# Retention into a gated feed-forward layer on one core: early decayed values and masks, both state products behind the row transposes, group 1 by halves, chunk 1 placed later

## The chip, the cores and the metric

The kernel runs on one core of a Trainium2 chip. Its engines are TensorE (PE, matrix products and transposes into PSUM), VectorE (DVE), ScalarE (ACT), GpSimd (POOL) and SyncE (SP), which run beside each other and wait for each other through semaphores; sixteen DMA engines move data. The metric is the device time of one execution in microseconds (us); a time given without more is the median of several runs. A profile covers one execution, from the first to the last instruction (its span).

## The reference, cut to what matters

Two layers in a row. The first is a recurrence over 768 positions for 4 batches and 8 heads of width 64; the second is a normalised, gated feed-forward layer (FFN) over the resulting 3072 rows of 512.

```python
# q, k, v: (4, 8, 768, 64); w_gate, w_val: (512, 1536); w_out: (1536, 512)
gamma = 1.0 - 2.0 ** (-5.0 - np.arange(H))
for t in range(S):
    state = gamma * state + outer(k[:, :, t], v[:, :, t])      # (B, H, D, D)
    y[:, :, t] = 1 / sqrt(D) * q[:, :, t] @ state
x = y.transpose(0, 2, 1, 3).reshape(B * S, H * D)
xn = x / sqrt(mean(x * x, axis=-1) + 1e-6) * rms_g
g = xn @ w_gate
out = (g * sigmoid(g) * (xn @ w_val)) @ w_out
```

## The kernel before

The kernel cuts the positions into 6 chunks of 128. Inside a chunk the recurrence becomes products: scores `a = k q^T` under a causal mask, their product with the values, and the query times the state that the earlier chunks left. The values are scaled by a decay (`vp`), the outputs by its inverse. A chunk has 4 batches of 128 rows, so 512 columns (`GT`) of the FFN; two batches are a group (`p` = 0 or 1). The FFN of a chunk is 12 tiles of hidden columns (`gv`) and 4 down-projections (`down`), and the attention of the next chunk is issued between these. The order of the calls is the order on every engine.

Chunk 0 uses masks that hold the decay already, so only its state needs the scaled values. The pieces that matter here:

```python
    ident_i = nc.vector.tensor_scalar(out=ident, in0=off, scalar1=0.0, scalar2=None, op0=ALU.is_equal)
    late_i = nc.vector.tensor_scalar(out=late, in0=offp_f, ...)     # offp comes from GpSimd
    nc.vector.tensor_tensor(out=reach, in0=offp_f, in1=late, op=ALU.add)

    def decays():              # ScalarE: four activations, vd_* scale values, yd_* scale outputs
        nc.scalar.activation(vd_p, va_p, AF.Exp, scale=-1.0, bias=zero)
        # ... vd_n, yd_p, yd_n likewise

    def vp_pair(c, p):         # GpSimd: the decayed values of a group
        nc.gpsimd.tensor_tensor(out=x, in0=u["v"]..., in1=vd_p[:, c]..., op=ALU.mult)

    def kvp(c, p):             # TensorE: 32 small products, the group's state product
        nc.tensor.matmul(u["kv"][b][t, hp * D:hp * D + D], u["k"][r, h, s], u["vp"][r, h, s], ...)

    def state0(p, eng): ...    # kv from PSUM to st_f
    def state_diag(p): ...     # GpSimd: st_f into the diagonal blocks of st_d (zero elsewhere)
    def state1(p): ...         # VectorE: st_f += kv
    def x_pe(c, p, j): ...     # TensorE: transposes of a normed batch;  x_copy: to SBUF
    def tp(c, p, n, a, eng):   # TensorE: transposes of q or k, and a copy
    def y1(p): ...             # TensorE: query times st_d, and masked scores times vp;  y1_out: scaled

    def gv(c, n0, n1, t0, t1): # hidden tiles n0..n1, columns t0..t1: two PSUM banks of products,
        for wt, name in ((wg_b, "g_ps"), (wv_b, "v_ps")):           # silu on ScalarE, times on VectorE
            ...
```

PSUM has eight banks, given out in turn; once `split[0]` is set, four go to the attention and four to the FFN. The order of chunk 0 and 1 (cut):

```python
    v_cast(0)
    # ... transposes of group 1's q, y0(0, 0), y0(0, 1)
    squares0(0)
    decays()
    # ... norm of group 0, scores of group 1
    load_w(5, 6)
    load_w(6, 8)
    gv(0, 0, 1, 0, 256)
    # ... gv 1, 2; y0 of group 1
    squares0(1); eps0(1); power(0, 1)
    vp_pair(0, 0)
    gv(0, 3, 4, 0, 256)
    norm0(1)
    gv(0, 4, 5, 0, 256)
    for n in "qk":
        load_pair(1, 0, n)
    load_w(8, 10)
    load_w(10, 12)
    gv(0, 5, 6, 0, 256)
    x_pe(0, 1, 0); x_pe(0, 1, 1); # ... and their copies
    load_pair(1, 0, "v", after=i)
    kvp(0, 0)
    vp_pair(0, 1)
    for p in range(2):
        nc.gpsimd.memset(st_d[p], 0.0)
    gv(0, 0, 2, 256, 512)
    state0(0, "a")
    for i in range(3):
        load_wo(4 * i, 4 * i + 4)
    gv(0, 2, 4, 256, 512)
    state_diag(0)
    kvp(0, 1)
    # ... VectorE: causal_p, causal (two tensor_scalar)
    gv(0, 4, 6, 256, 512)
    # ... gv 6 to 11, and chunk 1's group 0 between them
    norm(1, 0, 0, 1)
    down(0, 0); down(0, 1)
    x_pe(1, 0, 0); # ... x_copy, x_pe(1, 0, 1), x_copy
    # ... tp(1, 1), vp_pair(1, 1), down(0, 2), ap(1, 1), ap_mask, down(0, 3), t_dma(2, 0), t_dma(2, 1)

    steps = [L(gv, 1, n, n + 2, t, t + 256) for t in (0, 256) for n in (0, 2, 4, 6)]
    steps += [L(gv, 1, n, n + 1, 0, GT) for n in range(8, NFF)]
    steps += [L(down, 1, b) for b in range(B)]
    y1(1); y1_out(1); kvp(1, 1)
    split[0] = True
    run(steps, {...})          # step number -> attention of chunk 2, issued after that step
    for c in range(2, NCH):
        steps = [L(gv, c, n, n + 1, 0, GT) for n in range(NFF)]
        ...
```

Of the kernel before, what the change touches and what calls it, by code (L numbers as in the profile page):

```python
# [16 lines left out]
def kernel(  # L17
# [11 lines left out]
    nc = tc.nc  # L29
# [10 lines left out]
    GT = B * C  # L40
# [36 lines left out]
    def load_w(n0, n1):  # L77
        sl = slice(n0 * 128, n1 * 128)
        nc.gpsimd.dma_start(out=wg_b[:, :, sl], in_=wg_v[:, :, sl])
        nc.gpsimd.dma_start(out=wv_b[:, :, sl], in_=wv_v[:, :, sl])  # L80
# [62 lines left out]
    mhalf = const.tile([128, 2], F32, name="mhalf")  # L143
    nc.vector.memset(mhalf, -0.5)
    ident = const.tile([128, 128], BF16, name="ident")
    ident_i = nc.vector.tensor_scalar(out=ident, in0=off, scalar1=0.0, scalar2=None, op0=ALU.is_equal)

    late = const.tile([128, 256], F32, name="late")
    offp_f = offp.rearrange("p e f j -> p (e f j)")
    late_i = nc.vector.tensor_scalar(out=late, in0=offp_f, scalar1=0.0, scalar2=1.0e7, op0=ALU.is_lt, op1=ALU.mult)  # L150
    reach = const.tile([128, 256], F32, name="reach")
    nc.vector.tensor_tensor(out=reach, in0=offp_f, in1=late, op=ALU.add)


    mask0 = [[work.tile([128, 2, 256], F32, name="mask0", tag="v_f", bufs=6) for i in range(2)] for a in range(2)]
# [29 lines left out]
    def decays():  # L185
        nc.scalar.activation(vd_p, va_p, AF.Exp, scale=-1.0, bias=zero)
        nc.scalar.activation(vd_n, va_n, AF.Exp, scale=-1.0, bias=zero)
        nc.scalar.activation(yd_p, ya_p, AF.Exp, scale=1.0, bias=lnscale)
        nc.scalar.activation(yd_n.rearrange("p c i a -> p c a i"), va_n.rearrange("p c (a i) -> p c a i", i=2),
                             AF.Exp, scale=1.0, bias=lnscale)  # L190

    causal_p = const.tile([128, 256], BF16, name="causal_p")
    causal = const.tile([128, 128], BF16, name="causal")
    st_f = [const.tile([128, 2, NHP, D], F32, name=f"st_f{p}") for p in range(2)]
    st_b = [const.tile([128, 2, NHP, D], BF16, name=f"st_b{p}") for p in range(2)]

    st_d = [const.tile([128, 2, NHP, 2 * D], BF16, name=f"st_d{p}") for p in range(2)]

    def heat(n):
        hot = bank("hot")  # L200
        for _ in range(n):
            nc.tensor.matmul(hot, ones[:, :128], ones, start=True, stop=True)  # L202
# [49 lines left out]
    def v_cast(p):  # L252
        u = U[0, p]
        u["vb"] = work.tile([128, H, 2 * D], BF16, name="vb", bufs=2)
        nc.scalar.copy(u["vb"], u["v"])

    def vp_pair(c, p):
        u = U[c, p]
        x = work.tile([128, H * 2, D], BF16, name="vp2", bufs=3)
        nc.gpsimd.tensor_tensor(  # L260
            out=x, in0=u["v"].rearrange("p h (e d) -> p (h e) d", e=2),
            in1=vd_p[:, c].rearrange("p h e -> p (h e)")[:, :, None].to_broadcast([128, 2 * H, D]), op=ALU.mult)
        u["vp"] = x.rearrange("p (h e) d -> p h (e d)", e=2)
# [319 lines left out]
    tc_(0, 1, "q", 0, "v")  # L583
    tc_(0, 1, "q", 1, "v")
    squares0(0)
    decays()
    tp(0, 1, "k", 0)
    tp(0, 1, "k", 1)
    eps0(0)
# [25 lines left out]
    squares0(1)  # L615
    eps0(1)
    power(0, 1)
    vp_pair(0, 0)
    gv(0, 3, 4, 0, 256)
    norm0(1)  # L620
    gv(0, 4, 5, 0, 256)
    for n in "qk":
        load_pair(1, 0, n)
    load_w(8, 10)
    load_w(10, 12)
    gv(0, 5, 6, 0, 256)
    x_pe(0, 1, 0)
    x_pe(0, 1, 1)
# [1 line left out]
    i = x_copy(0, 1, 1, "a")  # L630
    load_pair(1, 0, "v", after=i)
    kvp(0, 0)
    vp_pair(0, 1)
    for p in range(2):
        nc.gpsimd.memset(st_d[p], 0.0)
    gv(0, 0, 2, 256, 512)
    state0(0, "a")
    for i in range(3):
        load_wo(4 * i, 4 * i + 4)
    gv(0, 2, 4, 256, 512)  # L640
    state_diag(0)
    kvp(0, 1)
    nc.vector.tensor_scalar(out=causal_p, in0=offp_f, scalar1=0.0, scalar2=None, op0=ALU.is_ge)
    nc.vector.tensor_scalar(out=causal, in0=off, scalar1=0.0, scalar2=None, op0=ALU.is_ge)
    gv(0, 4, 6, 256, 512)
    state0(1, "a")
    vp_pair(1, 0)
    gv(0, 6, 7, 0, GT)
    state_diag(1)
    for n in "qk":  # L650
        load_pair(1, 1, n)
    gv(0, 7, 8, 0, GT)
    for n, e in (("q", "a"), ("k", "v")):
        for a in range(2):
            tp(1, 0, n, a, e)
    load(2, 0)
    i = gv(0, 8, 9, 0, GT)
    load_pair(1, 1, "v", after=i)
    begin(1)
    ap(1, 0, 0)  # L660
    ap(1, 0, 1)
# [3 lines left out]
    kvp(1, 0)  # L665
    ap_mask(1, 0, 1, 0)
    ap_mask(1, 0, 1, 1)
    state1(0)
    gv(0, 10, 11, 0, GT)
    y1(0)  # L670
    gv(0, 11, 12, 0, GT)
    y1_out(0)
# [1 line left out]
    square(1, 0, 1)  # L674
    rstd(1, 0)
    state_cast(0)
    load(2, 1)
    norm(1, 0, 0, 1)
    down(0, 0)
    down(0, 1)  # L680
    x_pe(1, 0, 0)
    x_copy(1, 0, 0, "v")
    x_pe(1, 0, 1)
    x_copy(1, 0, 1, "v")
    for n, e in (("q", "a"), ("k", "v")):
        for a in range(2):
            tp(1, 1, n, a, e)
    vp_pair(1, 1)
    load(2, 2)
    down(0, 2)  # L690
    ap(1, 1, 0)
    ap(1, 1, 1)
    for a in range(2):
# [24 lines left out]
    run(steps, {
        0: [L(square, 1, 1, 0), L(square, 1, 1, 1), L(rstd, 1, 1), L(state1, 1), L(state_cast, 1),
            L(vp, 2, 0), L(vp, 2, 1)],  # L720
        1: [L(norm, 1, 1, 0, 1), L(begin, 2), L(load, 3, 0)],
        2: [L(x_pe, 1, 1, 0), L(x_copy, 1, 1, 0, "v"), L(x_pe, 1, 1, 1), L(x_copy, 1, 1, 1, "a"), L(load, 3, 1),
            L(t_dma, 2, 2), L(t_dma, 2, 3)],
        4: [L(a_pair, 2, 0), L(a_mask, 2, 0, 0)],
        5: [L(a_mask, 2, 0, 1), L(a_mask, 2, 1, 0), L(vp, 2, 2), L(vp, 2, 3)],
        6: [L(a_mask, 2, 1, 1)],
        7: [L(values, 2, 0), L(load, 3, 2), L(t_dma, 3, 0), L(t_dma, 3, 1)],
        8: [L(y_out, 2, 0, 0), L(y_out, 2, 0, 1), L(load, 3, 3)],
        9: [L(state_add, 2, 0), L(a_pair, 2, 1), L(square, 2, 0, 0), L(a_mask, 2, 2, 0)],
        10: [L(a_mask, 2, 2, 1), L(a_mask, 2, 3, 0), L(square, 2, 0, 1), L(rstd, 2, 0), L(state_cast, 0)],  # L730
        11: [L(a_mask, 2, 3, 1), L(norm, 2, 0, 0, 1), L(x_dma, 2, 0, 0), L(x_dma, 2, 0, 1)],
        12: [L(values, 2, 1), L(y_out, 2, 1, 0), L(y_out, 2, 1, 1), L(square, 2, 1, 0), L(square, 2, 1, 1),
             L(rstd, 2, 1), L(norm, 2, 1, 0, 1), L(x_dma, 2, 1, 0), L(x_dma, 2, 1, 1),
             L(state_add, 2, 1), L(state_cast, 1), L(vp, 3, 0), L(vp, 3, 1)],
        13: [L(load, 4, 0), L(t_dma, 3, 2), L(t_dma, 3, 3)],
        14: [L(a_pair, 3, 0), L(a_mask, 3, 0, 0, 1), L(a_mask, 3, 1, 0, 1)],
    })

    for c in range(2, NCH):
        steps = [L(gv, c, n, n + 1, 0, GT) for n in range(NFF)]  # L740
        steps += [L(down_last if (c, b) == (NCH - 1, B - 1) else down, c, b) for b in range(B)]
        d = c + 1
        more = d + 1 < NCH
        more2 = d + 2 < NCH
        after = {}
        if d < NCH:
            after = {
                0: [L(begin, d)] + [L(load, d + 1, 1)] * more,
                1: [L(values, d, 0), L(vp, d, 2), L(vp, d, 3)],
                2: [L(y_out, d, 0, 0)],  # L750
                3: [L(y_out, d, 0, 1)] + [L(state_add, d, 0)] * more,
                4: [L(square, d, 0, 0)],
                5: [L(a_pair, d, 1), L(a_mask, d, 2, 0), L(square, d, 0, 1), L(rstd, d, 0)]
                   + [L(state_cast, 0), L(load, d + 1, 2)] * more,
                6: [L(a_mask, d, 2, 1), L(norm, d, 0, 0), L(x_dma, d, 0, 0)]
                   + [L(t_dma, d + 1, 0)] * more,
                7: [L(norm, d, 0, 1), L(x_dma, d, 0, 1), L(a_mask, d, 3, 0)]
                   + [L(vp, d + 1, 0), L(vp, d + 1, 1), L(t_dma, d + 1, 1)] * more,
                8: [L(a_mask, d, 3, 1)] + [L(load, d + 1, 3)] * more,
                9: [L(values, d, 1)],  # L760
                10: [L(y_out, d, 1, 0)],
                11: [L(y_out, d, 1, 1), L(square, d, 1, 0), L(square, d, 1, 1), L(rstd, d, 1)],
                12: [L(norm, d, 1, 0, 1), L(x_dma, d, 1, 0), L(x_dma, d, 1, 1)]
                    + [L(state_add, d, 1), L(state_cast, 1)] * more
                    + [L(load, d + 2, 0)] * more2 + [L(t_dma, d + 1, 2), L(t_dma, d + 1, 3)] * more,
                13: [L(a_pair, d + 1, 0), L(a_mask, d + 1, 0, 0, 1), L(a_mask, d + 1, 1, 0, 1)] * more,
            }
        run(steps, after)
# [28 lines left out]
```

## Time and profile before

| | before |
|---|---|
| median of 3 runs | 254.52 us (252.93 to 255.78) |
| span of the profiled execution | 252.0 us |
| PE busy | 229.9 us, 91% of the span |
| DVE, ACT, POOL busy | 128.5, 86.6, 116.1 us |
| granted TensorE clock, mean | 0.976 of full speed |
| DMA | 30.48 MB, mean 121 GB/s |

The page shows the span in 40 slices of 6.3 us, with the busy tenths of each engine, and the granted TensorE clock. The list of waits gives, for an instruction's line and the line that released it, the total, the number and the longest. The timeline gives start and duration of instructions, merged where equal ones follow each other; a bracket gives the idle time before, and what ended it. L289 is `kvp`, L260 `vp_pair`, L350 `x_pe`, L517 the products of `gv`, L445 the scores of chunks 2 to 5, L300 `state1`, L496 the addition of the state in later chunks.

### The profile page before, as it was taken

The page shows a single profiled execution, that of the slowest core. Times are in us where ns is not written, and L with a number is a line of the kernel's source. Part 1 is how long each engine was busy: PE and PEld are TensorE (multiplying, and loading weights), DVE is VectorE, ACT ScalarE, POOL GpSimd, SP SyncE. Part 2 cuts the span into 40 slices and gives each one's busy share as a digit, 9 for nine tenths or more (in the row PEclk, how much of TensorE's full clock was granted, in tenths as well). Part 3 has the DMA queues.
Part 4 walks back from the last instruction along what each step waited for, and adds up shares of the span by engine and source line. Part 5 has one row for each costly group of instructions (what it writes and reads, how often), then busy time and mean ns, then how long its engine had stood idle before and what let it go on. Part 6 is the DMA issues. An engine that isn't in the chain of part 4 may idle for free. (4 is left out here: it accounts for less than half of the span.)

```text
span 252.0 us, 5095 instructions
## 1 busy us (share of the span) xinstructions
PE 229.9 (91%) x2050; PEld 122.4 (49%) x2050; DVE 128.5 (51%) x219; ACT 86.6 (34%) x173; POOL 116.1 (46%) x151
## 2 busy tenths in 40 slices
PE   5966839996988999999999999999999999999993
PEld 1444735553576844545454445454444444444442
DVE  2487462566547657464694615675526852144300
ACT  2747403423242332322424133423135323333220
POOL 7945999907929942178391670681400101000000
PEclk9799976999999999999999999999999999999998
DMA  8999999997997999559899499399650103300022
GB/s 102 167 198 156 124 209 194 190 199 92 174 212 101 118 135 170 109 104 158 157 116 176 95 122 194 69 139 125 142 165 3 23 18 82 128 0 0 3 83 85
DMA packets 87799, 30.48 MB, mean 121 GB/s; under 512 B 73696, under 2 KB 83680, under 8 KB 87776
## 3 DMA queue, kind: packets, MB, share of 16 engines
q0 software_dynamic: 53040, 15.21, 62.3%
q1 hardware_dynamic: 34064, 14.82, 30.9%
q8 instruction: 16, 0.26, 0.4%
q10 hardware_dynamic: 672, 0.13, 0.3%
q14 instruction: 7, 0.06, 0.1%
HBM read 28.58 MB, written 6.29 MB: 138 GB/s over the span
## 5 line engine op out<-in xcount | busy, mean ns | idle before, releaser
L522 DVE TENSOR_TENSOR hT<-sg,v_ps 128x512 bf16<-128x512 bf16 (+1 forms) x75 | 49.8, 664 | 82.8 <-PE v_ps L517 80.0
L517 PE MATMUL g_ps<-xnT,wg_b 128*128 128x512 bf16 (+1 forms) x344 | 76.2, 350 | 2.3 <-DVE am L247 0.9
L517 PE MATMUL v_ps<-xnT,wv_b 128*128 128x512 bf16 (+1 forms) x344 | 75.4, 348 | 1.7 <-DMA wv_b<-in_moe_w_val_dram 0.7
L521 ACT ACTIVATE sg<-g_ps 128x512 bf16<-128x512 f32 (+1 forms) x75 | 43.4, 580 | 89.7 <-PE g_ps L517 88.5
L536 PE MATMUL o_ps<-wo_b,hT 128*128 128x512 bf16 x276 | 61.6, 379 | 0.0
L517 PEld LDWEIGHTS <-wv_b 128*128 128x128 bf16 x344 | 33.9, 99 | 31.6 <-DMA wv_b<-in_moe_w_val_dram 1.2
L517 PEld LDWEIGHTS <-wg_b 128*128 128x128 bf16 x344 | 32.5, 99 | 29.2 <-DMA wg_b<-in_moe_w_gate_dram 1.6
L536 PEld LDWEIGHTS <-hT 128*128 128x128 bf16 x276 | 26.5, 98 | 31.6
L414 POOL TENSOR_SCALAR m<-ms 128x2 f32<-128x2 f32 x10 | 2.2, 218 | 77.2 <-ACT xsq L409 77.2
L538 ACT COPY o_sb<-o_ps 128x512 f32<-128x512 f32 x23 | 13.4, 581 | 42.6 <-PE o_ps L536 42.6
L422 DVE SCALAR_TENSOR_TENSOR xn<-x,rstd,g_bc 128x512 bf16<-128x512 f32 x20 | 19.1, 982 | 12.3 <-POOL rstd L330 12.3
L454 DVE TENSOR_TENSOR am<-a_ps,causal 128x512 bf16<-128x512 f32 x32 | 20.9, 682 | 0.0
L428 POOL TENSOR_TENSOR vp<-v_f,vd_n 128x512 bf16<-128x512 f32 x16 | 18.2, 1169 | 0.0
L409 ACT ACTIVATE xsq<-x 128x512 bf16<-128x512 f32 x20 | 12.4, 623 | 9.4 <-DVE x L400 7.7
L104 POOL DMA_DIRECT2D v_f<-in_v_dram x16 | 14.7, 917 | 1.3 <-DMA qb<-in_q_dram 1.3
L107 POOL DMA_DIRECT2D qb<-in_q_dram x16 | 15.0, 937 | 0.1
L107 POOL DMA_DIRECT2D kb<-in_k_dram x16 | 14.4, 899 | 0.0
L400 DVE TENSOR_TENSOR x<-y_ps,yd_n 128x512 f32<-128x512 f32 x16 | 10.8, 684 | 1.1 <-PE y_ps L490 1.1
L202 PE MATMUL hot<-ones 128*128 128x512 bf16 x22 | 7.7, 492 | 1.4 <-DVE ones L135 1.4
L260 POOL TENSOR_TENSOR vp<-v2f,vd_p 128x1024 bf16<-128x1024 f32 x4 | 8.4, 2099 | 0.1
L445 PE MATMUL a_ps<-qT,kT 64*128 64x128 bf16 x128 | 5.9, 218 | 2.4 <-DVE st_f L496 1.8
L308 POOL CAST st_b<-st_f 128x512 bf16<-128x512 f32 x8 | 4.8, 605 | 6.5 <-DVE st_f L496 6.5
(87 smaller groups left out, 160.3 us busy)
## 6 DMA issues: line engine op xcount, KB each, us to landing
v_f<-in_v_dram POOLq DMA_DIRECT2D x16, 256.0 KB, 8.0
out_dram<-o_sb SPq DMA_DIRECT2D x15, 256.0 KB, 2.3
out_dram<-o_sb SPq DMA_DIRECT2D x17, 128.0 KB, 3.9
v2f<-in_v_dram SPq DMA_DIRECT2D x8, 256.0 KB, 5.7
qb<-in_q_dram POOLq DMA_DIRECT2D x16, 128.0 KB, 4.9
kb<-in_k_dram POOLq DMA_DIRECT2D x16, 128.0 KB, 8.0
wo_b<-in_moe_w_out_dram POOLq DMA_DIRECT2D x3, 512.0 KB, 8.8
q2b<-in_q_dram POOLq DMA_DIRECT2D x8, 128.0 KB, 5.1
```

The source lines that it names most:

```text
L104: nc.gpsimd.dma_start(out=x, in_=unit_v[n][c, b])
L107: nc.gpsimd.dma_start(out=x.rearrange("p (h d) -> p h d", h=H), in_=unit_v[n][c, b])
L400: nc.vector.tensor_tensor(out=x[:, :, :, i, :], in0=u["y"][i].rearrange("p (b a d) -> p b a d", b=2, a=NHP), in1=yd_n[:, c, i][:, None, :, ...
L409: nc.scalar.activation(xsq, u["x"][:, b], AF.Square, scale=1.0 / math.sqrt(DM), accum_out=u["ms_"][:, b:b + 1])
L422: nc.vector.scalar_tensor_tensor(out=u["xn"][b], in0=u["x"][:, b], scalar=u["rstd"][:, b:b + 1], in1=g_bc, op0=ALU.mult, op1=ALU.mult)
L428: nc.gpsimd.tensor_tensor(out=x, in0=U[c, b]["v"], in1=vd_n[:, c, :, None].to_broadcast([128, H, D]), op=ALU.mult)
L454: nc.vector.tensor_tensor(out=x, in0=u["a_ps"][i].rearrange("p (a t) -> p a t", a=NHP), in1=causal[:, None, :].to_broadcast([128, NHP, 128 ...
L517: nc.tensor.matmul(x[:, o:o + w], wt[:, s, n * 128:(n + 1) * 128], XT[c][:, s, t0:t1], start=s == 0, stop=s == KS - 1)
L521: nc.scalar.activation(sg[:, :m], ps[0][:, :m], AF.Silu)
L522: return nc.vector.tensor_tensor(out=HT[c][:, n0:n1, t0:t1], in0=sg[:, :m].rearrange("p (n t) -> p n t", t=w), in1=ps[1][:, :m].rearrange( ...
L536: nc.tensor.matmul(ps, HT[c][:, n, b * C:(b + 1) * C], wo_b[:, n, :], start=n == 0, stop=n == NFF - 1)
L538: nc.scalar.copy(o_sb, ps)
```

## The change

Five parts. (1) `decays` and both `vp_pair` calls of chunk 0 are issued earlier, where GpSimd and ScalarE have gaps. (2) The zeros of `st_d` are written by VectorE at the start, in place of GpSimd later, and the two causal masks are made there too. (3) Both state products of chunk 0, `kvp(0, 0)` and `kvp(0, 1)`, follow the row transposes of group 1, and the loads of chunk 1 and of the last weights move up behind them. (4) Chunk 1's FFN is done in halves of 256 columns in all its tiles, and in chunks 2 to 5 the first four tiles are. (5) Chunk 1's work is placed later among the FFN's steps: its row transposes behind a third down-projection, its second group's outputs behind the first FFN step. It is meant to take the waits of TensorE in chunks 0 and 1 off its path.

```diff
+    st_d = [const.tile([128, 2, NHP, 2 * D], BF16, name=f"st_d{p}") for p in range(2)]
+    for p in range(2):
+        nc.vector.memset(st_d[p], 0.0)
     ... late, reach ...
+    nc.vector.tensor_scalar(out=causal_p, in0=offp_f, scalar1=0.0, scalar2=None, op0=ALU.is_ge)
+    nc.vector.tensor_scalar(out=causal, in0=off, scalar1=0.0, scalar2=None, op0=ALU.is_ge)
     ...
     v_cast(0)
+    decays()
+    vp_pair(0, 0)
     ...
     squares0(0)
-    decays()
     ...
     load_w(6, 8)
+    vp_pair(0, 1)
     gv(0, 0, 1, 0, 256)
     ...
     power(0, 1)
-    vp_pair(0, 0)
-    gv(0, 3, 4, 0, 256)
-    norm0(1)
-    gv(0, 4, 5, 0, 256)
     for n in "qk":
         load_pair(1, 0, n)
     load_w(8, 10)
     load_w(10, 12)
+    gv(0, 3, 4, 0, 256)
+    norm0(1)
+    gv(0, 4, 5, 0, 256)
     gv(0, 5, 6, 0, 256)
     ... x_pe, x_copy ...
     kvp(0, 0)
-    vp_pair(0, 1)
-    for p in range(2):
-        nc.gpsimd.memset(st_d[p], 0.0)
+    kvp(0, 1)
     gv(0, 0, 2, 256, 512)
     state0(0, "a")
+    state_diag(0)
     ... load_wo ...
     gv(0, 2, 4, 256, 512)
-    state_diag(0)
-    kvp(0, 1)
-    ... causal_p, causal ...
-    gv(0, 4, 6, 256, 512)
     state0(1, "a")
     vp_pair(1, 0)
+    for n in "qk":
+        load_pair(1, 1, n)
+    gv(0, 4, 6, 256, 512)
     ... v of chunk 1's group 1 is loaded after gv 10 in place of gv 8 ...
     down(0, 0)
+    load(2, 1)
     down(0, 1)
+    vp_pair(1, 1)
+    down(0, 2)
+    ... tp(1, 1) ...
     ... x_pe(1, 0, 0), x_copy, x_pe(1, 0, 1), x_copy ...
-    ... tp(1, 1) ...
-    vp_pair(1, 1)
     load(2, 2)
-    down(0, 2)
     ap(1, 1, 0)
     ...
-    steps = [L(gv, 1, n, n + 2, t, t + 256) for t in (0, 256) for n in (0, 2, 4, 6)]
-    steps += [L(gv, 1, n, n + 1, 0, GT) for n in range(8, NFF)]
+    steps = [L(gv, 1, n, n + 2, t, t + 256) for t in (0, 256) for n in range(0, NFF, 2)]
-    y1(1); y1_out(1); kvp(1, 1)
     run(steps, {
+        0: [y1(1), y1_out(1), kvp(1, 1)],
+        1: [square(1, 1, 0), square(1, 1, 1), rstd(1, 1), state1(1)],
+        2: [begin(2), norm(1, 1), state_cast(1), vp(2, 0), vp(2, 1), t_dma(2, 2), t_dma(2, 3)],
+        3: [load(3, 0)],
+        4: [x_pe(1, 1, 0), x_copy, x_pe(1, 1, 1), x_copy, load(3, 1)],     # was behind step 2
+        5: [a_pair(2, 0), a_mask],                                          # was 4
+        ...
+        8: [values(2, 0), load(3, 2), t_dma(3, 0), t_dma(3, 1)],            # was 7
+        9: [y_out(2, 0, 0), y_out(2, 0, 1), state_add(2, 0), load(3, 3)],
+        10: [a_pair(2, 1), ...],                                            # was 9
+        12: [values(2, 1), norm(2, 0), x_dma, ..., y_out(2, 1), state_add(2, 1), squares, norm(2, 1), ...],
     })
     for c in range(2, NCH):
-        steps = [L(gv, c, n, n + 1, 0, GT) for n in range(NFF)]
+        steps = [L(gv, c, n, n + 2, t, t + 256) for t in (0, 256) for n in (0, 2)]
+        steps += [L(gv, c, n, n + 1, 0, GT) for n in range(4, NFF)]
```

More of the change, by code (lines that the diff above doesn't have):

```diff
@@ L145 @@
     ident = const.tile([128, 128], BF16, name="ident")
-    ident_i = nc.vector.tensor_scalar(out=ident, in0=off, scalar1=0.0, scalar2=None, op0=ALU.is_equal)
+    nc.vector.tensor_scalar(out=ident, in0=off, scalar1=0.0, scalar2=None, op0=ALU.is_equal)
+    st_d = [const.tile([128, 2, NHP, 2 * D], BF16, name=f"st_d{p}") for p in range(2)]
+    for p in range(2):
+        nc.vector.memset(st_d[p], 0.0)
     late = const.tile([128, 256], F32, name="late")
@@ L152 @@
     nc.vector.tensor_tensor(out=reach, in0=offp_f, in1=late, op=ALU.add)
+    causal_p = const.tile([128, 256], BF16, name="causal_p")
+    nc.vector.tensor_scalar(out=causal_p, in0=offp_f, scalar1=0.0, scalar2=None, op0=ALU.is_ge)
+    causal = const.tile([128, 128], BF16, name="causal")
+    nc.vector.tensor_scalar(out=causal, in0=off, scalar1=0.0, scalar2=None, op0=ALU.is_ge)
     mask0 = [[work.tile([128, 2, 256], F32, name="mask0", tag="v_f", bufs=6) for i in range(2)] for a in range(2)]
@@ L190, in decays @@
                              AF.Exp, scale=1.0, bias=lnscale)
-    causal_p = const.tile([128, 256], BF16, name="causal_p")
-    causal = const.tile([128, 128], BF16, name="causal")
     st_f = [const.tile([128, 2, NHP, D], F32, name=f"st_f{p}") for p in range(2)]
     st_b = [const.tile([128, 2, NHP, D], BF16, name=f"st_b{p}") for p in range(2)]
-    st_d = [const.tile([128, 2, NHP, 2 * D], BF16, name=f"st_d{p}") for p in range(2)]
     def heat(n):
@@ L640 @@
     gv(0, 2, 4, 256, 512)
-    state_diag(0)
-    kvp(0, 1)
-    nc.vector.tensor_scalar(out=causal_p, in0=offp_f, scalar1=0.0, scalar2=None, op0=ALU.is_ge)
-    nc.vector.tensor_scalar(out=causal, in0=off, scalar1=0.0, scalar2=None, op0=ALU.is_ge)
-    gv(0, 4, 6, 256, 512)
     state0(1, "a")
     vp_pair(1, 0)
+    for n in "qk":
+        load_pair(1, 1, n)
+    gv(0, 4, 6, 256, 512)
     gv(0, 6, 7, 0, GT)
     state_diag(1)
-    for n in "qk":
-        load_pair(1, 1, n)
     gv(0, 7, 8, 0, GT)
@@ L656 @@
     load(2, 0)
-    i = gv(0, 8, 9, 0, GT)
-    load_pair(1, 1, "v", after=i)
+    gv(0, 8, 9, 0, GT)
     begin(1)
@@ L667 @@
     ap_mask(1, 0, 1, 1)
+    i = gv(0, 10, 11, 0, GT)
+    load_pair(1, 1, "v", after=i)
     state1(0)
-    gv(0, 10, 11, 0, GT)
     y1(0)
@@ L676 @@
     state_cast(0)
-    load(2, 1)
     norm(1, 0, 0, 1)
     down(0, 0)
+    load(2, 1)
     down(0, 1)
+    vp_pair(1, 1)
+    down(0, 2)
+    for n, e in (("q", "a"), ("k", "v")):
+        for a in range(2):
+            tp(1, 1, n, a, e)
     x_pe(1, 0, 0)
@@ L684 @@
     x_copy(1, 0, 1, "v")
-    for n, e in (("q", "a"), ("k", "v")):
-        for a in range(2):
-            tp(1, 1, n, a, e)
-    vp_pair(1, 1)
     load(2, 2)
-    down(0, 2)
     ap(1, 1, 0)
@@ L708, in L @@
         return lambda: f(*a)
-    steps = [L(gv, 1, n, n + 2, t, t + 256) for t in (0, 256) for n in (0, 2, 4, 6)]
-    steps += [L(gv, 1, n, n + 1, 0, GT) for n in range(8, NFF)]
+    steps = [L(gv, 1, n, n + 2, t, t + 256) for t in (0, 256) for n in range(0, NFF, 2)]
     steps += [L(down, 1, b) for b in range(B)]
-    y1(1)
-    y1_out(1)
-    kvp(1, 1)
     split[0] = True
     run(steps, {
[L719 to L732, printed above, removed]
@@ new lines @@
+        0: [L(y1, 1), L(y1_out, 1), L(kvp, 1, 1)],
+        1: [L(square, 1, 1, 0), L(square, 1, 1, 1), L(rstd, 1, 1), L(state1, 1)],
+        2: [L(begin, 2), L(norm, 1, 1, 0, 1), L(state_cast, 1), L(vp, 2, 0), L(vp, 2, 1), L(t_dma, 2, 2),
+            L(t_dma, 2, 3)],
+        3: [L(load, 3, 0)],
+        4: [L(x_pe, 1, 1, 0), L(x_copy, 1, 1, 0, "v"), L(x_pe, 1, 1, 1), L(x_copy, 1, 1, 1, "a"), L(load, 3, 1)],
+        5: [L(a_pair, 2, 0), L(a_mask, 2, 0, 0)],
+        6: [L(a_mask, 2, 0, 1), L(a_mask, 2, 1, 0), L(vp, 2, 2), L(vp, 2, 3)],
@@ new lines @@
+        7: [L(a_mask, 2, 1, 1)],
+        8: [L(values, 2, 0), L(load, 3, 2), L(t_dma, 3, 0), L(t_dma, 3, 1)],
+        9: [L(y_out, 2, 0, 0), L(y_out, 2, 0, 1), L(state_add, 2, 0), L(load, 3, 3)],
+        10: [L(a_pair, 2, 1), L(square, 2, 0, 0), L(a_mask, 2, 2, 0), L(a_mask, 2, 2, 1), L(state_cast, 0)],
+        11: [L(square, 2, 0, 1), L(rstd, 2, 0), L(a_mask, 2, 3, 0), L(a_mask, 2, 3, 1)],
+        12: [L(values, 2, 1), L(norm, 2, 0, 0, 1), L(x_dma, 2, 0, 0), L(x_dma, 2, 0, 1),
+             L(y_out, 2, 1, 0), L(y_out, 2, 1, 1), L(state_add, 2, 1), L(square, 2, 1, 0), L(square, 2, 1, 1),
@@ L733 @@
              L(rstd, 2, 1), L(norm, 2, 1, 0, 1), L(x_dma, 2, 1, 0), L(x_dma, 2, 1, 1),
-             L(state_add, 2, 1), L(state_cast, 1), L(vp, 3, 0), L(vp, 3, 1)],
+             L(state_cast, 1), L(vp, 3, 0), L(vp, 3, 1)],
         13: [L(load, 4, 0), L(t_dma, 3, 2), L(t_dma, 3, 3)],
```

## The prediction

> **What bounds the kernel now.** I read the page's slices first, then TensorE's waits, then the timeline around the longest one. Two rows of the slices (6.3 us each):
>
> ```profile
> PE   5966839996988999999999999999999999999993
> ...
> PEclk9799976999999999999999999999999999999998
> DMA  8999999997997999559899499399650103300022
> ```
>
> From slice 18 (113 us) on TensorE is full: 134.8 us busy of the 140 after 112 us. No rearrangement brings much there. The holes are in slices 1 to 13, chunks 0 and 1, and the clock row sinks in slices 5 and 6. The DMA row is at 9 for most of that time: keep it in mind. TensorE's waits, four of the fifteen rows (total, times, longest):
>
> ```profile
> PE kv_ps L289 <- POOL vp L260: 3.8, 1, 3.8
> PE x_ps L350 <- DVE xn L422: 3.0, 2, 1.9
> ...
> PE a_ps L445 <- DVE st_f L496: 1.8, 3, 0.9
> ...
> PE v_ps L517 <- DVE st_f L300: 0.6, 1, 0.6
> ```
>
> The longest is group 1's state product, `kvp(0, 1)`, which waits for GpSimd's decayed values. The timeline there (start, duration; us):
>
> ```profile
> 32.26 0.79 POOL L79 DMA_DIRECT2D wg_b<-in_moe_w_gate_dram  x1
> 32.99 0.80 POOL L80 DMA_DIRECT2D wv_b<-in_moe_w_val_dram  x1
> 33.40 1.27 DVE L643 TENSOR_SCALAR causal_p<-offp 128x256 bf16<-128x256 int32 x1
> 33.75 2.67 POOL L260 TENSOR_TENSOR vp<-v2f,vd_p 128x1024 bf16<-128x1024 f32 x1
> 34.59 1.91 DVE L644 TENSOR_SCALAR causal<-off 128x128 bf16<-128x128 int32 x1
> 36.37 1.91 POOL L635 MEMSET st_d<- 128x1024 bf16 x2
> 36.47 0.64 PE L289 MATMUL kv_ps<-vp,k2b 64*64 64x64 bf16 x32 [3.78 <-POOL vp L260]
> 37.04 1.89 PE L517 MATMUL g_ps<-xnT,wg_b 128*128 128x256 bf16 x8
> 38.73 1.91 PE L517 MATMUL v_ps<-xnT,wv_b 128*128 128x256 bf16 x8
> ...
> 40.43 1.73 PE L517 MATMUL g_ps<-xnT,wg_b 128*128 128x512 bf16 x4
> ...
> 42.00 1.03 PE L517 MATMUL v_ps<-xnT,wv_b 128*128 128x512 bf16 x4
> ```
>
> GpSimd reached `vp` only after issuing the loads of chunk 1 and the weights. The wait also has a tail: starts of equal banks lie 1.69, 1.70 and 1.57 us apart (37.04, 38.73, 40.43, 42.00), where elsewhere they lie 0.87 apart. The windows name it (busy us of PE, PEld, DVE, ACT, POOL; clock; DMA; GB/s):
>
> ```profile
> 34.00:42.00 8.00, 5.53 (x53) 3.53 (x52) 3.19 (x3) 1.14 (x3) 7.85 (x9) 0.57 1.43 197
> 42.00:60.00 18.00, 18.00 (x205) 9.02 (x203) 9.98 (x17) 6.46 (x13) 10.29 (x14) 1.00 1.26 171
> ```
>
> **What the Trainium skill says.** "TensorE: Matmul & The Clock Gate", Part 1 (the HAM clock gate): after an idle window of about 3.4 us the clock falls to half, and it returns after sustained work. The trace agrees: 3.78 us idle, clock 0.57 over the window, banks at half pace for three banks. "SBUF — State Buffer", Who interferes with whom: VectorE and GpSimd share a port pair that one instruction holds whole; `tensor_scalar` can be among the holders. The trace agrees: causal_p and causal took 1.27 and 1.91 beside a 2.67 vp, while the similar late (128x256) and ident (128x128) took 0.29 and 0.23 alone, and other vps 1.9. "VectorE: DVE Perf Modes", Zero memsets: a memset costs a cycle per element whatever the type. The 128x512 ones memset took 0.48 us, so I estimate 0.97 for each 128x1024 one. "DMA: Bandwidth & Descriptors", Issuing engines are not separate DMA queues: all issuers share the same 16 engines. The row of 9s with three issuers active fits.
>
> **The change, part by part.**
>
> *Decayed values early.* After its weight issue GpSimd is idle from 12.20 to 15.79 (3.59, ended by the norm). `decays` after `v_cast` can start on ScalarE at 11.91, is 4 small activations (14.73 to 15.73 before, so 1.0), and ScalarE's next work came at 14.15: free. vp(0,0) then runs from about 12.3 for 1.9 to 2.7 and ends by 15.0, ahead of the norm at 15.79: free. vp(0,1) goes behind `load_w(6, 8)` (issued by 22.4) and ends by 24.4, or 25.1 at the slow 2.67; the next norm on GpSimd comes at 25.46, and its values have landed at 14.3 + 6.6 = 20.9. Free. GpSimd's later queue loses 1.9 + 2.67 of vp and 1.91 of memset. So chunk 1's q and k loads move from 27.98 to about 26.1, the last weights from 30.75 to 29, and `wo` from 38.23 to about 33.5.
>
> *Zeros and masks early.* VectorE is idle from 3.47 to 5.32, 1.85 us. Two memsets of 0.97 make 1.94, so `late` moves by about 0.1. causal_p and causal, some 0.5 together when alone, then end near 6.7, ahead of the copy at 7.42. Up to 0.1 us.
>
> *Both state products behind the row transposes.* They are ready at 28.2, where TensorE next waits 0.37 for the copies of xnT. `kvp(0, 1)`, 0.35 warm, fills that wait. What goes: the wait of 3.78; the slow banks, (1.69 + 1.70 + 1.57) - 3 x 0.87 = 2.35; the product at its slow place, 0.57. What comes: nothing. Sum 6.7 us.
>
> *Chunk 1 placed later.* `x_pe(1, 0)` waits for the norm: the whole 3.0 row is one wait of 1.91 at 62.51 and one of 1.05 at 78.85. Behind `down(0, 2)` (2.6) and the 1.0 of transposes the first has 3.6 more us; behind two more steps of 1.73 less the later y1 (1.4) the second still has about 2. Both go: 3.0. The 0.64 wait for state1 (bank) at 74.65 goes too, as `kvp(1, 1)` moves a step away: starts there are 1.68 apart against 0.87, so 0.8.
>
> *Group 1 by halves.* Eight 256-wide matmuls start 0.87 us per bank, four 512-wide ones 0.86: the form costs nothing. It lets group 1 be needed two steps later in chunk 1 and its transfer two half-steps later in chunks 2 to 5. There I see no xnT wait now, so I count 0.
>
> *Chunk 2's attention.* The last row but one, 1.8 in three, is a_pair waiting for state_add. Its 0.93 in chunk 1 stays, I think: y_out and state_add now both follow the silu product of step 9, about 0.95 + 1.29 + 0.68 = 2.9 us after that step's matmuls, and a_pair comes after 1.73 of them. The 0.37 at the end of chunk 1 goes, since state_add runs before the norms.
>
> Sum: 6.7 + 3.0 + 0.8 + 0.4 - 0.1 = 10.8 us.
>
> **Rivals.**
>
> *The transfers become the bound.* With TensorE 7 us earlier from 33 us on, the weights must be there. In the kernel before, wv_b of tiles 8 to 9 was issued at 31.5 and landed 8.6 later, at 40.1; that of 10 to 11 at 33.0 + 9.8 = 42.8; `wo` at 45.3, about 47.8 and 51.5. Moving all by the 1.8 us that GpSimd gains (DMA is full at 195 GB/s, so more than that is not safe) gives 38.3, 41.0 and 49.7. By my new order they are needed at 39.5, 43.9 and, third part of wo, 49.4. So it fits with 1 to 3 us, the last about even. For chunk 2 it is tighter: 28 to 82 us moved 32 x 171 + 22 x 157 = 8,900 KB, and the same must now pass in about 43 + 1.8 us, 199 GB/s, which is what the full windows show (194 to 202). The transposed loads of batches 2 and 3 landed up to 10.8 us after issue, at 92.3, and were used at 93.3. This speaks for new waits of 0 to 4 us at a_pair of chunk 2; I charge 1. If it is worse, and an idle stretch long enough halves the clock again, half of the gain is lost: 249.
>
> *The gain is absorbed by norms.* If vp on GpSimd, in early time, holds the shared port against VectorE, or runs over 15.8, then the first norm moves and all behind it by as much: up to 1 us. Against it: VectorE's work there reads PSUM, and am stayed at 0.68 beside a vp (20.9 to 26). It would make 245.5.
>
> *Only the first wait goes.* If y1 inside the split banks, now between steps of the FFN, makes TensorE wait for VectorE (its queue then holds 4 masks, 2 outputs, 2 norms), chunk 1's 3.8 us come back as others: 248.
>
> *Everything counts and nothing comes back:* 243.7.
>
> **Range and chances.** 10.8 less 1.0 for transfers is 9.8; from the median 254.5 that is 244.7, and from the profiled span 252.0 it is 242.2. The lower end is 10.8 plus another 2.5 of small issue gaps that I haven't listed between 28 and 96 us: 241. The upper end is the first rival in full: 249. A gain of over 2% means below 249.4. Only a combination of rivals misses that: 0.89 faster, 0.09 within, 0.02 slower.
>
> **What would show it.** Right: vp(0,0) near 12.3 and vp(0,1) near 22.5; no wait of kv_ps; PEclk 9 in slices 5 and 6; the first down-projection near 48 instead of 54.7; x_ps waits under 0.5 in all; down of chunk 1 near 87 to 88 instead of 98.5; from there on the same spacing. Wrong: waits of g_ps, v_ps or o_ps on weights between 35 and 50, or of a_ps on qT or kT near 72 and 84, a later first norm than 15.8, or a low clock digit behind such a wait.

## The result and the profile after

| | before | changed |
|---|---|---|
| median | 254.07 us (252.93 to 255.78) | 246.70 us (244.58 to 247.76) |
| span of the profiled execution | 252.0 us | 243.8 us |
| mean granted TensorE clock | 0.976 | 0.993 |

The ratio is 0.9694, 95% interval 0.96 to 0.9788. The prediction was 244.7 us, range 241 to 249.

The three rows of the page's slices (6.1 us each here) that answer to those of before:

```profile
PE   5776999999999999995999999999999999999993
...
PEclk9999999999999999999899999999999999999999
DMA  8999999999989994999994998898540204200022
```

The holes of chunks 0 and 1 are closed: TensorE is full from slice 4 on (24 us; slices are counted from 0). But one hole is new, slice 18 (near 111 us), with a lower clock digit behind it. TensorE's waits name it (total, times, longest; two rows of eleven):

```profile
PE a_ps L449 <- DMA kT<-kb: 3.0, 1, 3.0
...
PE a_ps L449 <- DVE st_f L500: 1.3, 3, 0.5
```

Neither a wait of kv_ps nor one of x_ps for a norm is left. The early parts in the timeline of the changed kernel:

```profile
3.52 1.02 DVE L150 MEMSET st_d<- 128x512 uint32 x2
...
5.33 0.29 DVE L154 TENSOR_SCALAR late<-offp 128x256 f32<-128x256 int32 x1 [0.78 <-POOL offp L127]
...
12.40 1.90 POOL L264 TENSOR_TENSOR vp<-v2f,vd_p 128x1024 bf16<-128x1024 f32 x1
...
22.03 1.98 POOL L264 TENSOR_TENSOR vp<-v2f,vd_p 128x1024 bf16<-128x1024 f32 x1
...
27.56 0.74 PE L293 MATMUL kv_ps<-vp,k2b 64*64 64x64 bf16 x64
```

Both state products run in one piece, 64 matmuls, with no wait. How far the changed kernel is ahead follows from the same instruction in both timelines:

| start of | before | changed | ahead |
|---|---|---|---|
| first hidden tile of chunk 0 | 18.91 | 18.51 | 0.4 |
| first down-projection of chunk 0 | 54.90 | 47.38 | 7.5 |
| first down-projection of chunk 1 | 98.67 | 86.22 | 12.5 |
| first hidden tile of chunk 2 | 111.55 | 98.53 | 13.0 |
| first down-projection of chunk 2 | 135.50 | 127.37 | 8.1 |
| first down-projection of chunk 3 | 171.25 | 163.22 | 8.0 |

So 13.0 us are won by the end of chunk 1, and 4.9 are lost again within chunk 2. The timeline there, TensorE alone:

```profile
110.34 0.40 PE L449 MATMUL a_ps<-qT,kT 64*128 64x128 bf16 x8
113.70 0.40 PE L449 MATMUL a_ps<-qT,kT 64*128 64x128 bf16 x8 [2.96 <-DMA kT<-kb]
114.03 1.26 PE L521 MATMUL g_ps<-xnT,wg_b 128*128 128x512 bf16 x4
115.08 1.91 PE L521 MATMUL v_ps<-xnT,wv_b 128*128 128x512 bf16 x4
116.78 1.69 PE L521 MATMUL g_ps<-xnT,wg_b 128*128 128x512 bf16 x4
118.31 1.03 PE L521 MATMUL v_ps<-xnT,wv_b 128*128 128x512 bf16 x4
```

The scores of chunk 3's batch 3 wait 2.96 us for the transposed load of k. Behind that, bank starts lie 1.05, 1.70 and 1.53 us apart in place of 0.87 three times: 1.7 us more. It is the pattern of the old wait over again, idle time and then a slow clock, 4.6 us in all.

The transposed loads of batches 2 and 3 of chunk 3 are `t_dma(3, 2)` and `t_dma(3, 3)`, four entries on SyncE's queue. Of the last one I compare issue and landing, counted from the start of chunk 2's first hidden tile, with the moment at which TensorE had done the scores of batch 2 and was free for those of batch 3:

| | issue | to landing | landed | TensorE free for batch 3 | scores of batch 3 begin |
|---|---|---|---|---|---|
| before | 115.29, +3.7 | 8.1 | +11.8 | +12.0 | +12.0 |
| changed | 103.50, +5.0 | 10.2 | +15.1 | +12.2 | +15.2 |

The lines of the kernel before, then that of the changed one:

```profile
115.29 1.32 SPq L436 DMA_TRANSPOSE kT<-kb  x1
...
123.29 0.62 PE L445 MATMUL a_ps<-qT,kT 64*128 64x128 bf16 x16
```

```profile
103.50 2.03 SPq L440 DMA_TRANSPOSE kT<-kb  x1
```

In the kernel before, the transfer came in about as it was needed: a slack of 0.15 us that showed as no wait. The list of waits before did hold a hint that the prediction passed over, L445 waiting once for kT, 0.6 us at 177. The change took 3.3 us from the transfer, 1.2 by a later issue and 2.1 by a longer way. The later issue has a visible neighbour. First the changed kernel's second pair of norms of chunk 1, then that of the kernel before:

```profile
94.12 2.52 DVE L426 SCALAR_TENSOR_TENSOR xn<-x,rstd,g_bc 128x512 bf16<-128x512 f32 x2 [1.97 <-POOL rstd L334]
94.61 2.93 POOL L432 TENSOR_TENSOR vp<-v_f,vd_n 128x512 bf16<-128x512 f32 x2
```

```profile
106.57 1.42 DVE L422 SCALAR_TENSOR_TENSOR xn<-x,rstd,g_bc 128x512 bf16<-128x512 f32 x2 [2.57 <-POOL rstd L330]
...
109.28 2.05 POOL L428 TENSOR_TENSOR vp<-v_f,vd_n 128x512 bf16<-128x512 f32 x2
```

With `state_add` moved ahead of the norms, GpSimd's vp of chunk 3 runs beside them, and both are slower. The transposes of xn wait for these norms, and the transposed loads stand behind them in SyncE's queue.

### The profile page after: what moved, and what is told of

Read it like the earlier page. It is cut to its first block, busy times and chain, and to the rows that moved or that the text cites. A ratio compares the mean times of both kernels' runs of the same rounds, so it can differ in the third digit from the quotient of the medians.

```text
span 243.8 us, 5417 instructions
## 1 busy us (share of the span) xinstructions
PE 227.2 (93%) x2210; PEld 136.6 (56%) x2210; DVE 125.6 (52%) x221; ACT 86.4 (35%) x173; POOL 114.6 (47%) x149
## 5 line engine op out<-in xcount | busy, mean ns | idle before, releaser
L521 PE MATMUL g_ps<-xnT,wg_b 128*128 128x256 bf16 (+1 forms) x424 | 75.8, 313 | 1.7 <-DMA wg_b<-in_moe_w_gate_dram 0.9
L521 PE MATMUL v_ps<-xnT,wv_b 128*128 128x256 bf16 (+1 forms) x424 | 75.6, 313 | 1.2 <-DMA wv_b<-in_moe_w_val_dram 0.8
L521 PEld LDWEIGHTS <-wv_b 128*128 128x128 bf16 x424 | 41.5, 98 | 23.3 <-DMA wv_b<-in_moe_w_val_dram 1.7
L521 PEld LDWEIGHTS <-wg_b 128*128 128x128 bf16 x424 | 40.0, 98 | 22.1 <-issue 1.9
L426 DVE SCALAR_TENSOR_TENSOR xn<-x,rstd,g_bc 128x512 bf16<-128x512 f32 x20 | 17.6, 908 | 11.7 <-POOL rstd L334 11.7
L432 POOL TENSOR_TENSOR vp<-v_f,vd_n 128x512 bf16<-128x512 f32 x16 | 19.0, 1217 | 0.0
L413 ACT ACTIVATE xsq<-x 128x512 bf16<-128x512 f32 x20 | 12.5, 624 | 9.4 <-DVE x L404 7.7
L404 DVE TENSOR_TENSOR x<-y_ps,yd_n 128x512 f32<-128x512 f32 x16 | 10.8, 684 | 0.6 <-PE y_ps L494 0.6
L264 POOL TENSOR_TENSOR vp<-v2f,vd_p 128x1024 bf16<-128x1024 f32 x4 | 7.7, 1917 | 3.9 <-DMA v2f<-in_v_dram 3.1
L449 PEld LDWEIGHTS <-kT 64*128 64x128 bf16 x128 | 3.8, 94 | 8.0 <-issue 4.9
```

The costliest lines, as they stand in the source:

```text
L404: nc.vector.tensor_tensor(out=x[:, :, :, i, :], in0=u["y"][i].rearrange("p (b a d) -> p b a d", b=2, a=NHP), in1=yd_n[:, c, i][:, None, :, ...
L413: nc.scalar.activation(xsq, u["x"][:, b], AF.Square, scale=1.0 / math.sqrt(DM), accum_out=u["ms_"][:, b:b + 1])
L426: nc.vector.scalar_tensor_tensor(out=u["xn"][b], in0=u["x"][:, b], scalar=u["rstd"][:, b:b + 1], in1=g_bc, op0=ALU.mult, op1=ALU.mult)
L432: nc.gpsimd.tensor_tensor(out=x, in0=U[c, b]["v"], in1=vd_n[:, c, :, None].to_broadcast([128, H, D]), op=ALU.mult)
L521: nc.tensor.matmul(x[:, o:o + w], wt[:, s, n * 128:(n + 1) * 128], XT[c][:, s, t0:t1], start=s == 0, stop=s == KS - 1)
```

## The experiments

Four theories were tested. Theory A: the loss lies in the place that the transposed loads have in SyncE's queue. Theory B: the DMA engines are full, and any order only moves the wait. Theory C: the loads of chunk 4 beside them make them slow to land. Theory D: vp holds the norms back. Times before, run on the same chips: 254.2 us (first four), 253.9 (next four), 253.45 (last four). Executions more than 1.5% above the fastest of the same kernel are left out of the medians from here on, and as the profiles of chunk 1 alone and of the loads held back are of such executions, only the place of waits and the landings are read from these two.

**The changed kernel again**, unedited.

> The changed kernel once more, beside its variants on one chip. Both theories: 245 to 248 us. The wait of a_ps for kT of chunk 3 is there again at 2 to 4 us near 111, and the first eight down-projections keep the same spacing; the low clock behind it may come or not.

247.88 us, ratio 0.9749 (0.9688 to 0.9809). The wait for kT is there: 4.0 in two, the longest 3.3, and the clock was at 0.50 from 116 to 118. The loss is no chance of one profile.

**Transposed loads early.**

```diff
-        13: [load(4, 0), t_dma(3, 2), t_dma(3, 3)],
+        11: [t_dma(3, 2), t_dma(3, 3), ...],
+        13: [load(4, 0)],
```

> The transposed loads of batches 2 and 3 of chunk 3 are issued three steps earlier (behind step 11 of chunk 1, ahead of the transposes of xn and the stores on SyncE's queue). Theory A (the wait near 111 is the place in that queue: issued at 99 to 105.5, they have 5 us to land where they take 8 to 11): the wait of 3.0 us and the slow clock behind it go, the span falls by 3 to 4.8 us to about 239.5, the time to 241 to 243. Theory B (the 16 DMA engines are saturated over the whole of chunks 0 to 2, and a transfer that is moved forward only pushes another back): a new wait of 2 to 4 us for xnT near 102 or for other transfers, and the time stays within 1.5 us of the changed kernel.

243.10 us, ratio 0.9566 (0.9485 to 0.9647). The wait for kT is gone, but another took its place:

```profile
101.21 1.55 PE L521 MATMUL g_ps<-xnT,wg_b 128*128 128x256 bf16 x8 [2.61 <-DMA xnT<-xn]
102.56 1.91 PE L521 MATMUL v_ps<-xnT,wv_b 128*128 128x256 bf16 x8
```

The queue was worked off in order. SyncE could issue the last transposed load only at 92.75, behind an idle queue since 91.33, because its input `kb` landed at 92.70, and the transposes of xn behind it began at 95.90 in place of 90.84. A was right about kT and wrong about the price. The new wait comes from that order, so it does not show that the DMA engines were full; B is neither shown nor excluded here.

**Calls of the loads later.**

```diff
-        13: [load(4, 0), ...]           # and load(4, 1) behind step 0 of chunk 2
+        4: [..., load(4, 0), load(4, 1)]      # of chunk 2
```

> The loads of batches 0 and 1 of chunk 4 (1 MB by destination, six transfers on GpSimd's queue) are issued behind step 4 of chunk 2 in place of 97 to 103 us, so that nothing but stores runs beside the transposed loads of chunk 3. Theory A (place in the queue alone): those still are issued at 99 to 105 and take 8 to 11 us, the wait stays at 2 to 3 us, time 245 to 248. Theory C (contention: they take 10 us because six loads run beside them): landing falls to 3 to 5 us, the wait goes to 0, the span falls by 3 to 4.8, time 241 to 243, unless the later loads make a new wait.

242.03 us, ratio 0.9522 (0.9472 to 0.9572); the wait for kT was 0.7, the landing took 8.2, and the clock did not fall. But the loads moved only from 97.49 to 99.70: GpSimd has nothing to wait for, so a later call behind idle steps is not a later issue. It merely did vp(3, 2) and vp(3, 3) first. The experiment shows that the wait hangs on a small margin, not what it was designed for.

**State addition back.**

```diff
-  y_out(2, 1), state_add(2, 1), squares, rstd, norm(2, 1), x_dma, state_cast(1), vp(3, 0), vp(3, 1)
+  y_out(2, 1), squares, rstd, norm(2, 1), x_dma, state_add(2, 1), state_cast(1), vp(3, 0), vp(3, 1)
```

> Only the state addition of group 1 in chunk 1 goes back behind the second pair of norms, as before the change, and with it the cast and GpSimd's vp(3, 0) and vp(3, 1). Theory D (vp on GpSimd holds the shared port against those norms, which took 2.52 us together in place of 1.42, and so delays all that follows in SyncE's queue by 1.1): the norms take 1.4, the transposed loads are issued 1.1 us earlier, the wait falls from 3.0 to about 2, a wait of 0.4 for st_f comes back; the time falls by 0.7, or by up to 2.4 if the shorter wait leaves the clock at full. Theory A without D: no difference beyond 0.5 us.

244.50 us, ratio 0.9608 (0.9554 to 0.9662). The norms took 1.42 together, the last transposed load was issued at +3.7 as before the change, the wait fell to 1.7 and the clock stayed at 1.00 behind it. So the later issue is due to the new place of the state addition. D is a part of that: with the loads first (below) the norms also take 1.41, with the addition still ahead of them, and the issue is at +4.3, 0.7 earlier than in the changed kernel. The other 0.6 is a lead of TensorE: the norms start 4.4 us ahead of chunk 2 in both of these, and 5.0 ahead before and with the addition put back, where the scores still wait for st_f. The landing stayed at 10.2, so the longer way is not D.

**No halves in chunks 2 to 5.**

```diff
-        steps = [gv(c, n, n + 2, t, t + 256) for t in (0, 256) for n in (0, 2)] + [gv(c, n, n + 1, 0, GT) for n in range(4, NFF)]
+        steps = [gv(c, n, n + 1, 0, GT) for n in range(NFF)]
```

> The changed kernel without the halves in chunks 2 to 5 (each hidden tile over all 512 columns). The prediction counted 0 for the halves. If that holds: the same time as the changed kernel within 0.7 us, no wait for xnT at 98 to 99. If the halves cover for group 1's later norms in chunk 1: xnT lands at about 99 against a start at 98.5, a wait of 0.5 to 1 us appears there, and since it moves the scores of chunk 3 back by as much, the wait for kT shrinks by as much and the total is still the same within 0.5.

247.67 us, ratio 0.9707 (0.9625 to 0.979), as the changed kernel. A wait of 0.54 for xnT appears where it was expected; the wait for kT stayed at 3.0. The halves there hide half a microsecond and bring nothing to the total that these runs show. The wait for kT did not shrink by that half microsecond, as expected of it: that transfer landed 11.0 after its issue, in place of 10.2.

**Chunk 0 alone** (parts 1 to 3; all behind hidden tile 7 as before).

> Parts 1 to 3 alone: chunk 0 as in the changed kernel up to hidden tile 7, everything behind it as before. The prediction's own steps: the state product's wait of 3.78 us and the slow clock go, 6.7 us, so 247.5 us. The changed trace, which was 7.5 us ahead at the first down-projection: 246.5 us. If the transfers give it back even here (rival): 250 to 253, with waits on weights or on transposed loads of chunk 2 or 3.

247.38 us, ratio 0.9713 (0.9637 to 0.979): 6.5 us less than before (5.3 to 9.2 by the interval), where the prediction's step was 6.7. No wait for kT of more than 0.5. It is as fast as the whole change.

**Chunk 1 alone** (chunk 0 as before; all behind hidden tile 7 as changed).

> Parts 4 and 5 alone: everything from hidden tile 8 of chunk 0 on as in the changed kernel, chunk 0 as before. The prediction's own steps: 3.0 + 0.8 + 0.4 = 4.2 us, so 250 us. The changed trace gained 5.5 us between its first down-projection and the end of chunk 1, then lost 4.8 at chunk 3's transposed loads: if that loss belongs to the placement of chunk 1's last steps it comes here too, and the time is 253 to 254.5; if it comes only because chunk 0 runs ahead of the transfers, there is no such wait and the time is 248 to 250.

Of its four runs one counts, 250.14 us (the others: 253.93, 255.79, 256.25), which gives no verdict. Its trace has the waits for kT of chunk 3, 0.96 and 3.03. Chunk 0 alone had none over 0.5. So they belong to the placement of chunk 1's last steps, not to chunk 0's lead.

**The old wait filled.**

```diff
     state_diag(0)
+    heat(17)       # 17 products of a constant, unused
     kvp(0, 1)
```

> The kernel before with 17 idle products (3.7 us of TensorE work on a constant, result unused) ahead of the second state product, so that TensorE is busy while GpSimd makes the values. The wait itself stays. If the slow banks behind the wait are the clock's answer to the idle time: the clock stays at full from 34 to 42, banks are 0.87 apart, and the time falls by 2.4 us to 251.7. If they are slow for another reason (transfers of the weights, VectorE): no change, 254.

253.60 us over 20 runs, ratio 0.9994 (0.9966 to 1.0021): no gain. Yet its timeline has the step that was meant, and the windows (columns as in the prediction) show where it went in this execution:

```profile
32.27 3.83 PE L202 MATMUL hot<-ones 128*128 128x512 bf16 x17
36.64 0.44 PE L289 MATMUL kv_ps<-vp,k2b 64*64 64x64 bf16 x32 [0.54 <-POOL vp L260]
...
52.54 5.34 PE L536 MATMUL o_ps<-wo_b,hT 128*128 128x512 bf16 x24
...
60.15 0.40 PE L350 MATMUL x_ps<-ident,xn 128*128 128x128 bf16 x4 [1.91 <-DVE xn L422]
61.49 4.42 PE L536 MATMUL o_ps<-wo_b,hT 128*128 128x512 bf16 x12
```

```profile
62.00:64.00 2.00, 2.00 (x6) 0.65 (x5) 0.13 (x1) 0.00 (x1) 2.00 (x3) 0.50 1.05 190
```

The clock was at 1.00 from 34 to 42, and the first down-projection began at 52.54 in place of 54.90: 2.36 us, as expected. Then the next wait, 1.91 us for the norm, had the slow clock behind it (0.50 from 62 to 64), and the down-projection there took from 61.49 to 65.84; at 98.17 the lead was 0.5 (98.67 before). So the slow banks do come from the idle time, but removing them alone bought nothing: the clock fell at the next wait. The last section shows why it could fall there.

**Loads first.** The loads of batch 0 of chunk 4 go to 88.7 to 91.4 us, those of batch 1 to 94.9 to 97.6, where the DMA share of the changed kernel was at 0.32 to 0.38 (it was above 0.9 from 88 to 92). They also keep vp off the norms.

```diff
+        11: [..., load(4, 0)],
-        12: [..., norm(2, 1), x_dma, state_cast(1), vp(3, 0), vp(3, 1)],
+        12: [..., norm(2, 1), x_dma, load(4, 1), state_cast(1), vp(3, 0), vp(3, 1)],
-        13: [load(4, 0), t_dma(3, 2), t_dma(3, 3)],
+        13: [t_dma(3, 2), t_dma(3, 3)],      # and no load(4, 1) in chunk 2
```

> The loads of batches 0 and 1 of chunk 4 are issued earlier, not later: those of batch 0 right behind step 11 of chunk 1 (near 88), those of batch 1 ahead of vp(3, 0) (near 94 to 97), where the DMA engines are at 0.3 to 0.5; vp(3, 0) then also keeps clear of the second norms. Theory C (contention of those six loads is what makes the transposed loads of chunk 3 land after 10 us): they land within 4 to 7 us, the norms take 1.4 us in place of 2.5, the transposed loads are issued 1 us earlier, the wait for kT is 0, span near 239.3, time 240.5 to 242. Theory A (issue place alone): the wait falls by the 1 us of the norms to about 2, time 244 to 246. A new wait for xnT at 98.5 of up to 1 us would show that the earlier loads got in the way of the transposes of xn.

241.92 us, ratio 0.9547 (0.9507 to 0.9587), span 239.8. The lines of VectorE, SyncE and TensorE that matter:

```profile
94.95 1.41 DVE L426 SCALAR_TENSOR_TENSOR xn<-x,rstd,g_bc 128x512 bf16<-128x512 f32 x2 [1.98 <-POOL rstd L334]
```

```profile
103.63 1.23 SPq L440 DMA_TRANSPOSE kT<-kb  x1
```

```profile
111.17 0.62 PE L449 MATMUL a_ps<-qT,kT 64*128 64x128 bf16 x16
```

The norms take 1.41, the last transposed load is issued at +4.3 (chunk 2 begins at 99.35) and lands 4.1 us later in place of 10.2, and the scores run in one piece. There is no wait for kT in the whole trace, and none for a transfer of xnT: the wait was not only moved, which speaks against B.

**Loads first, and the addition of the state ahead of the norms in chunks 2 to 4.**

```diff
-  12: [norm(d, 1), x_dma, x_dma, state_add(d, 1), state_cast(1), ...]
+  12: [state_add(d, 1), norm(d, 1), x_dma, x_dma, state_cast(1), ...]
```

> The same, and in chunks 2 to 4 the state addition of group 1 goes ahead of the two norms, so that the scores of the next chunk need not wait for it: the waits for st_f of 0.5, twice, go; the norms and their transposes come 0.7 later, which the halves cover. 0.9 us below the kernel with the loads first alone: 239.5 to 241.5. If the later transposes push the transposed loads of chunk 4 beyond their use (they landed 0.9 us ahead of it in the changed kernel), a wait for kT of up to 1 us near 149 takes the gain back.

240.96 us, ratio 0.9506 (0.9469 to 0.9543), the lowest median of all, though the interval overlaps that of the loads first alone. Both 0.5 waits for st_f are gone; one of 0.6 for xnT is there near 104.

**Chunk 1 alone with the loads first.**

> Chunk 0 as before, everything from hidden tile 8 of chunk 0 on as in the changed kernel, with the loads of chunk 4 issued first. If the placement of chunk 1 is worth the 4.2 to 5.5 us that its trace shows up to the end of chunk 1, and only the wait for kT of chunk 3 (3.0 and the slow clock) took them back: 249 to 250.5. If chunk 1 alone brings nothing for another reason: 252.5 to 255.

247.90 us, ratio 0.9775 (0.9739 to 0.9811): 5.6 us less than before, where the same without the moved loads gave no verdict. Chunk 1's placement is worth what its trace shows, once its own side effect is gone: from the first down-projection of chunk 0 to the first hidden tile of chunk 2 it takes 51.1 us (56.7 before, 51.2 in the changed kernel), so nearly all of the gain is there before the transposed loads of chunk 3 are needed. The transposed load landed in 4.3.

**Loads held back by a dependency.**

```diff
+  load(4, 0), load(4, 1): issued after the silu product of hidden tile 4 of chunk 2
```

> The loads of batches 0 and 1 of chunk 4 held back by a dependency on the silu product of hidden tile 4 of chunk 2 (near 107.5). Moving their calls alone had delayed them by only 2.2 us, since GpSimd had nothing to wait for. Theory C: no load of GpSimd's queue runs beside the transposed loads of chunk 3, so that these land 3 to 5.5 us after issue and the wait for kT there is 0; 240.5 to 242.5 if the late loads make no wait of their own (kT or vp of chunk 4 near 135 to 150). Theory A: still 8 us and more to land, a wait of 0.7 to 3.

243.80 us, ratio 0.9642 (0.9587 to 0.9696). Beside no loads the last transposed load landed in 3.8, and the wait near 111 is gone, as C has it. But chunk 4's own transposed loads came late: a wait of 4.0 for kT at 135.3. Later by 2.2 us (242.03) did as well as earlier (241.92); later by some 13 us, as here, made a new wait.

## Why the prediction was right or wrong

- **Decayed values early, free**: right. vp(0, 0) began at 12.40 (predicted 12.3), vp(0, 1) at 22.03 (22.5), and the norm behind them came at 15.38, no later than before. One reading was wrong: no vp ran from 20.9 to 26 in the kernel before (its first was at 26.13), so the 0.68 of `am` there showed nothing about a vp beside it.
- **Zeros and masks, 0.1 us**: wrong in size, without consequence. I took 0.97 per memset from the one of ones. The profile shows them as uint32 of half as many elements, 1.02 for both, the form that the Trainium skill describes in "VectorE: DVE Perf Modes", Zero memsets can be issued as uint32, and that the estimate left out. `late` came at 5.33 against 5.32.
- **State products, 6.7**: right. Chunk 0 alone measured 6.5; the trace is 7.5 ahead, 0.4 of it from before the first hidden tile.
- **Chunk 1 placed later, 3.8 and 0.4 of chunk 2's scores**: too small. The trace gains 5.5 from 47.4 to 98.5, the run of chunk 1 with the loads first 5.6. Of the excess of 1.3, 0.6 is the wait for st_f, which I had kept at 0.93 and which fell to 0.33. The rest is not small gaps: from 28 to 96 us the idle time outside the waits listed is 0.04, so the 2.5 of such gaps behind the lower end of the range are not there either. An estimate for the rest: a bank of products lasts 1.04 and the next starts 0.87 after it, so each wait that goes saves 0.17 beyond its idle time, 0.5 for the three of which I had counted the idle time alone.
- **Halves, 0**: right (247.67 without those of chunks 2 to 5).
- **The transfers, 1.0**: this is the step that failed. The down-projection of chunk 1 came at 86.2 (87 to 88 predicted), but the spacing behind it did not stay as it was. The transfers cost 4.9, in the form that I had described as a rival (a wait, then the slow clock), but one chunk later. I looked for it at chunk 2's scores because the bytes of 28 to 82 us had to pass sooner. What bound was no total of bytes (with the loads first the same bytes pass without a wait): one transfer had no slack in the kernel before, and the change issued it 1.2 later and it took 2.1 longer. The first follows from `state_add` before the norms, which is part of the change that I had credited with 0.4: shown by putting it back. The second goes when the six loads beside it go, whether earlier (4.1) or later (3.8): shown. Why it took 10.2 and not 8.1 with the same six loads beside it as before the change stays open; with the addition put back, loads and transposes had the order of before and it still took 10.2. It is not chance: with the old chunk 1 it took 8.0 to 9.1 in three traces, with the new one and all six loads in their place 10.2 to 11.3 in five.

Sum: 13.0 won, 4.9 lost, 8.1 in the profile and 7.4 in the medians, against the 9.8 predicted. With the loads first the whole change gains 11.5 in the medians, near the sum of its halves measured apart, 6.5 and 5.6. That the time of the change itself fell well inside the range is partly luck: 2.2 more was won than the 10.8 predicted, and 3.9 more lost than the 1.0 charged. Luck seems to decide the 1.7 of slow clock too: of the four runs of the changed kernel, the one with a granted clock of 0.999 took 244.58 us, where the other three, at 0.979 to 0.993, took 245.77 to 247.76.

## What to carry to other kernels

A wait that is not in the profile may have no slack: before moving work, compare landing and use of every transfer behind it, not only the waits that exist; a short wait of the same kind elsewhere is a hint. A call placed later is an issue placed later only if its engine has something to wait for; and in a queue that goes in order, one early entry that isn't ready holds all the others. When half of a change measures as much as the whole, look for what the other half gave back, and repair that.

## What the runs showed of the hardware that was not expected

- The clock does not fall by the length of one wait alone. All changes of the granted clock in a trace lie whole multiples of 3.41 us apart (before: 4.30, 7.71, 11.13, 35.02, 41.85). Of the 955 such steps that began at full clock in the fourteen traces, the 24 in which TensorE was idle for 1.87 us or more (nine of them near a kernel's end) were followed by half clock, and none with 1.73 or less was. So it counts where a wait lies. That of 1.91 in the kernel before (60.60 to 62.51) is cut by the end of a step at 62.33, and the clock stayed at 1.00; the same wait in the filled kernel (58.24 to 60.15) lies whole in the step from 58.05 to 61.46, and the clock fell at 61.46. Of the 2.96 for kT, 2.40 lie in the step that ended at 114.71, where the clock fell; of the 1.72 with the state addition back, 1.62 lie in one step, and it stayed. The Trainium skill ("TensorE: Matmul & The Clock Gate", Part 1) gives an idle window of about 3.4 us; here little more than half a step idle was enough.
- The last transposed load of chunk 3 (128 KB) landed in 3.0 to 4.3 us without the six loads of chunk 4 beside it (four traces), and in 8.0 to 11.3 with them (nine traces).
- The norms, with two inputs in SBUF, took 1.08 and 1.53 us beside vps of GpSimd and 0.75 each without, and the vps 1.48 each in place of 1.05 (the instructions of the pairs above).
